# Attention and low-rank mixer on one core: diagonal score blocks first, key copies ahead of the cast of u, both transposed operands through ScalarE, the U-product in four column groups, a new order of the loop after the start-up

## The chip, the cores and the metric

The kernel runs on one core of a Trainium2 chip. The metric is device time in microseconds (us) of one execution; profiles are of one execution each, on the same kind of chip, and their span is about 2 us shorter than the time. Five engines matter: PE (TensorE matmul; PEld is its weight load), ACT (ScalarE), DVE (VectorE), POOL (GpSimd) and the DMA engines. In these traces each engine executes its own instructions in the order in which the program issues them, and this kernel sets that order by hand. "Slow clock" and "fast clock" are names for two durations that the same PE work shows: the six U-product matmuls of a pair take 0.82 us in the start-up of the kernel before and 0.50 us later.

## The reference, cut to what matters

```python
# q, k, v: (4, 8, 768, 64); local causal window of 96, 8 global keys, per-head slope
scores = q @ k.T / sqrt(64) + bias;  scores = where(keep, scores, -1e9)
a = softmax(scores);  attn = a @ v                       # -> x: (4, 768, 512)
h = (x.transpose(0, 2, 1) @ U) @ V                       # U: (768, 32), V: (32, 768)
u = x + h.transpose(0, 2, 1)
out = u + relu(u @ w_ch1) @ w_ch2                        # 512 -> 2048 -> 512
```

Heads are handled in 16 pairs, `i = 0 .. 15`, four pairs to a batch element. A query block of 128 needs its own key block (the diagonal block) and the block before it (the previous block), in which the first 32 columns are replaced by the global keys.

## The kernel before

Every pair goes through the same steps: transpose q and k on PE (`tp`/`tpb`), evacuate them (`qT`, `kT`), copy keys for the previous blocks (`kP`), scores in three chunks (`sc`), exp (`ep`), mask, AV product (`ob`), normalise (`x_sb`), cast (`x16`), U-product (`tmp_ps`), V-product (`h_ps`), add into `x_sb`, cast of u (`uu`), transpose u (`tpu`), copy (`uT`). Two-matrix MLP work (`hps`, `cps`) is cut into pieces and put between these steps by `fill(f)` once a batch element is complete.

```python
def k_prev(i, eng):                     # needs kT
    eng.tensor_copy(kP[:, :, G:P], kT[:, 0:NPB, G:P])
    eng.tensor_copy(kP[:, :, 0:G], kT[:, 0:1, 0:G].broadcast_to((P, NPB, G)))

# ... (1, t): block before, needs kP; (0, t): diagonal, needs only kT
ORDER = [(1, t) for t in range(1, NSB)] + [(0, t) for t in range(1, NSB)] + [(0, 0)]
CH = [list(range(0, 4)), list(range(4, 8)), list(range(8, 11))]

def mix_h(i, eng):
    hps = ps_ob("h_ps")                 # the same PSUM buffer as the AV product, bufs=1
    # ... six matmuls with V
    nc.vector.tensor_tensor(xp, xp, hps[...], ALU.add)
    eng.tensor_copy(uu, xp)             # the cast of u

# start-up loop, pairs 0 to 3 (no MLP work exists yet), cut:
    scores(i + 1, 0); av(i); norm(i); scores(i + 1, 1)
    if i > 0: mix_t(i - 1)
    cast_x(i); mask(i + 1, 0)
    transposes(i + 2, 0); mix_tmp(i); scores(i + 1, 2); transposes(i + 2, 1)
    mix_h(i, nc.vector if i == 0 else nc.gpsimd)
    mask(i + 1, 1)
    k_prev(i + 2, nc.vector if i == 0 else nc.gpsimd)

# loop after the start-up, pairs 4 to 15 (f MLP pieces in each gap), cut:
    scores(i + 1, 0); fill(f); av(i); norm(i); fill(f)
    scores(i + 1, 1); cast_x(i); fill(f)
    mask(i + 1, 0); transposes(i + 2, 0); fill(f)
    mix_tmp(i); scores(i + 1, 2); fill(f)
    mix_h(i, nc.gpsimd); fill(f)
    transposes(i + 2, 1); mask(i + 1, 1); k_prev(i + 2, nc.gpsimd); fill(f)
    # ... loads
    mix_t(i); fill(f)
```

The softmax here doesn't subtract the row's maximum and nothing guards it: scores larger than these inputs give would overflow.

## Time and profile before

The median of the kernel before is 291.75 us (290.54 to 291.88, four runs). I cut its profile at two events that the timeline shows: the first MLP matmul, and the start of the MLP matmuls that then run to the end without attention between them.

| Stage of the profile before | from, us | to, us | length, us |
|---|---|---|---|
| start-up (pairs 0 to 3, no MLP) | 0 | 58.68 | 58.68 |
| middle (pairs 4 to 15 with MLP pieces) | 58.68 | 228.52 | 169.84 |
| tail (MLP only) | 228.52 | 289.3 | 60.78 |

The windows view of the kernel before, one stretch from the start-up and one from the middle. The columns are stretch, its length, busy us and instructions of PE, PEld, DVE, ACT and POOL, then granted clock, DMA share and GB/s. The DMA share is above 1 in places and is not used here.

```profile
30.00:40.00 10.00, 6.20 (x84) 4.74 (x80) 5.63 (x9) 4.72 (x10) 3.90 (x5) 1.00 1.22 118
120.00:140.00 20.00, 19.92 (x163) 9.50 (x161) 9.76 (x15) 7.16 (x13) 5.14 (x6) 1.00 0.66 86
```

In the start-up PE is idle for almost four tenths of the time and no other engine is full either. That is the mark of a chain of dependences, not of a busy engine. In the middle PE is full.

The view of PE's waits of the kernel before (what PE waited for, us in total, times, longest us):

```profile
PE sc L265 <- POOL kP L226: 8.4, 3, 3.4
PE sc L265 <- DVE kP L226: 6.8, 3, 3.6
...
PE tmp_ps L336 <- ACT qT L211: 3.2, 6, 0.7
PE tmp_ps L336 <- DMA u_111<-in_moe_U_dram: 1.9, 1, 1.9
PE tpu L365 <- DVE kT L215: 1.2, 6, 0.2
```

The key copy is about half of all that PE waits for (15.2 of 31.3 us, the whole view summed). The chain that ended last shows what lies behind the copy (start us, us, what), in one start-up iteration of the kernel before:

```profile
32.89 0.77 DVE kT L215
...
33.77 0.95 DVE x_sb L353
...
34.78 1.35 POOL uu L357
36.13 0.59 POOL kP L225
36.72 0.27 POOL kP L226
...
37.04 0.28 PE sc L265
```

The key copy at 36.13 us needs only kT, whose evacuation ends at 33.85 us in the timeline. It stood in POOL's queue behind the cast of u, which itself stood behind the addition of h on DVE. So the scores of the next pair waited for the mixer of the previous one.

### The profile page before, as it was taken

The numbers are of one execution on the slowest core, as the hardware profiler recorded it, in microseconds if no ns is written. First come the engines' busy times: TensorE is split into PE (matmuls) and PEld (weight loads), VectorE is DVE, ScalarE is ACT, GpSimd is POOL, SyncE is SP. The second block draws the span as 40 slices with busy tenths as digits, with TensorE's granted clock in tenths as the row PEclk, the third lists the DMA queues.
The fourth block names the chain that finished last, engine by engine and source line by source line (L and its number), as shares of the span: only waits on it lengthen the run. The fifth ranks groups of instructions, "written<-read, shape, count | busy, mean of one in ns | idle before, by whom it ended". The sixth has DMA issues, their size and how long they took to land.

```text
span 289.3 us, 5035 instructions
## 1 busy us (share of the span) xinstructions
PE 252.7 (87%) x2144; PEld 129.0 (45%) x2144; DVE 149.3 (52%) x239; ACT 104.4 (36%) x185; POOL 61.2 (21%) x80
## 2 busy tenths in 40 slices
PE   2564585698899999999999999988999999999994
PEld 1343464454444444444444444544444444444441
DVE  5646736736665665564554635666655432123221
ACT  2753552444644234533146331446431032013100
POOL 8820137102430721060200701120301100000000
PEclk9999999999999999999999999999999999999998
DMA  8999979960971294039120291200011200210021
GB/s 86 176 191 211 175 98 192 191 71 6 125 64 39 30 207 107 2 39 162 73 81 4 21 180 73 69 18 2 0 39 37 75 0 0 75 73 0 0 73 74
DMA packets 47975, 22.68 MB, mean 78 GB/s; under 512 B 31408, under 2 KB 44368, under 8 KB 47952
## 3 DMA queue, kind: packets, MB, share of 16 engines
q0 software_dynamic: 36656, 13.73, 41.1%
q1 hardware_dynamic: 11296, 8.63, 10.2%
q8 instruction: 17, 0.28, 0.4%
q14 instruction: 6, 0.05, 0.1%
HBM read 27.46 MB, written 6.29 MB: 117 GB/s over the span
## 4 chain that ended last, share of the span: by engine, by line
PE 64%; DVE 11%; ACT 10%; POOL 8%; DMA 3%; issue 2%; POOLq 0%; DVEq 0%
PE cps L399 25%; PE hps L381 21%; PE sc L265 6%; ACT ep L270 4%; DVE kT L215 4%; DMA u_111<-in_moe_U_dram 3%; DVE x_sb L353 3%; PE tmp_ps L336 3%; POOL kP L225 3%; PE h_ps L348 2%; PE ob L303 2%; PE ob L307 2%; ACT qT L211 1%; POOL qkst L98 1%; POOL uu L357 1%
## 5 line engine op out<-in xcount | busy, mean ns | idle before, releaser
L381 PE MATMUL hps<-uT,w_16_81 128*128 128x512 f16 x384 | 94.1, 383 | 0.4
L399 PE MATMUL cps<-w_16_82,htr 128*128 128x512 f16 x384 | 90.4, 380 | 0.0
L270 ACT ACTIVATE ep<-sc 128x512 f16<-128x512 f32 (+1 forms) x96 | 48.7, 560 | 90.0 <-PE sc L265 90.0
L381 PEld LDWEIGHTS <-w_16_81 128*128 128x128 f16 x384 | 34.2, 98 | 40.2 <-issue 5.1
L399 PEld LDWEIGHTS <-htr 128*128 128x128 f16 x384 | 34.4, 98 | 38.5
L386 ACT ACTIVATE htr<-hps 128x512 f16<-128x512 f32 x48 | 28.7, 598 | 62.5 <-PE hps L381 61.9
L388 DVE TENSOR_SCALAR htr<-hps 128x512 f16<-128x512 f32 x48 | 33.0, 688 | 34.6 <-PE hps L381 34.6
L357 POOL CAST uu<-x_sb 128x768 f16<-128x768 f32 x14 | 13.1, 935 | 146.9 <-DVE x_sb L353 146.9
L406 DVE TENSOR_TENSOR osb<-cps,x_sb 128x512 f32<-128x512 f32 x24 | 16.6, 690 | 34.0 <-PE cps L399 34.0
L283 DVE TENSOR_TENSOR ep<-ep,expb 128x1280 f16<-128x1280 f16 x32 | 26.2, 818 | 7.4 <-ACT ep L270 7.4
L265 PE MATMUL sc<-qT,kP 64*128 64x128 f16 x160 | 11.6, 249 | 16.2 <-POOL kP L226 8.4
L353 DVE TENSOR_TENSOR x_sb<-x_sb,h_ps 128x768 f32<-128x768 f32 x16 | 15.2, 951 | 16.6 <-PE h_ps L348 16.6
L203 PEld LDWEIGHTS <-qkst 128*64 128x64 f16 x384 | 14.6, 130 | 15.8 <-issue 10.2
L265 PEld LDWEIGHTS <-kP 64*128 64x128 f16 x160 | 5.9, 104 | 27.6 <-POOL kP L226 13.0
L319 DVE RECIPROCAL rcp<-ob 128x12 f32<-128x12 f32 x16 | 3.7, 232 | 25.2 <-PE ob L307 25.2
L225 POOL COPY kP<-kT 128x480 f16<-128x480 f16 x13 | 13.0, 1000 | 15.4 <-DVE kT L215 15.4
L320 DVE TENSOR_TENSOR x_sb<-ob,rcp 128x768 f32<-128x768 f32 x16 | 15.3, 957 | 0.6
L303 PE MATMUL ob<-vp_85,ep 128*128 128x65 f16 x160 | 15.0, 209 | 0.0
L307 PE MATMUL ob<-v_84,ep 128*128 128x65 f16 x160 | 14.9, 209 | 0.0
L203 PE MATMUL tpb<-ident_93,qkst 128*64 128x128 f16 x144 | 10.0, 314 | 5.3 <-DMA qkst<-in_q_dram 4.8
L303 PEld LDWEIGHTS <-ep 128*128 128x128 f16 x160 | 13.1, 108 | 1.6 <-issue 0.3
L307 PEld LDWEIGHTS <-ep 128*128 128x128 f16 x160 | 13.2, 109 | 0.0
(112 smaller groups left out, 204.1 us busy)
## 6 DMA issues: line engine op xcount, KB each, us to landing
out_dram<-osb SPq DMA_DIRECT2D x24, 256.0 KB, 2.0
qkst<-in_q_dram POOLq DMA_DIRECT2D x7, 384.0 KB, 5.6
qkst<-in_k_dram POOLq DMA_DIRECT2D x7, 384.0 KB, 8.3
v_84<-in_v_dram POOLq DMA_DIRECT2D x7, 384.0 KB, 11.3
w_16_81<-in_moe_w_ch_dram POOLq DMA_DIRECT2D x2, 1024.0 KB, 15.8
w_16_82<-in_moe_w_ch_dram POOLq DMA_DIRECT2D x2, 1024.0 KB, 13.4
vp_85<-v_84 SPq DMA_DIRECT2D x14, 121.9 KB, 3.0
vp_85<-v_84 SPq DMA_DIRECT2D x28, 20.3 KB, 2.5
```

The costliest lines, as they stand in the source:

```text
L203: nc.tensor.matmul(tp[64 * hi:64 * hi + 64, sb * P:(sb + 1) * P], stg[:, hi, sb], ident16, is_transpose=True, start=(sb == 0), stop=(sb == ...
L225: eng.tensor_copy(kP[:, :, G:P], kT[:, 0:NPB, G:P])
L265: nc.tensor.matmul(scs[hi][:, j * P:(j + 1) * P], lhsT, qT[r, t * P:(t + 1) * P], start=(j == 0), stop=(j == n - 1),)
L270: nc.scalar.activation(ep[:, hi, idx[0]:idx[0] + n].rearrange("p n c -> p (n c)"), scs[hi][:, 0:n * P], AF.Exp, scale=qk_scale,)
L283: nc.vector.tensor_tensor(blk, blk, eb[:, :, m:m + 1].broadcast_to((P, 2, NPB, P)), ALU.mult,)
L303: nc.tensor.matmul(ob[:, t], ep[:, hi, t - 1], vp16[:, i % VPR, hi, t - 1], start=True, stop=False,)
L307: nc.tensor.matmul(ob[:, t], ep[:, hi, NPB + t - 1], v16[:, i % VR, hi, t], start=False, stop=True,)
L353: nc.vector.tensor_tensor(xp, xp, hps[:, 0:S].rearrange("p (n c) -> p n c", n=NSB), ALU.add)
L381: nc.tensor.matmul(hh, w1_16[:, dc, jt * P:(jt + 1) * P], uT[:, dc, t0:t0 + TT], start=(dc == 0), stop=(dc == NDC - 1),)
L386: nc.scalar.activation(htr[:, jt], hh, AF.Relu)
L388: nc.vector.tensor_scalar_max(htr[:, jt], hh, 0.0)
L399: nc.tensor.matmul(cps, htr[:, jc, tt * P:(tt + 1) * P], w2_16[:, jc], start=(jc == 0), stop=(jc == NJC - 1),)
```

## The change

The intent is to shorten that start-up chain and to make PE's own attention work shorter. The diff, cut to its core (a switch `DT` for transposes by DMA is also added, but it is off and changes nothing):

```diff
-    load(2, 2)
     u16 = ...; nc.gpsimd.dma_start(u16, moe_U...)
-    v16w = cst.tile([R, S], FP16, name="v16w")
-    nc.gpsimd.dma_start(v16w, moe_V)
+    v16w = cst.tile([P, S], FP16, name="v16w")         # V four times, one per column group
+    nc.gpsimd.dma_start(v16w[0:R], moe_V)
+    for g in range(1, NGR):
+        nc.sync.dma_start(v16w[g * R:(g + 1) * R], v16w[0:R])
+    load(2, 2)
@@ kT evacuation
-            nc.vector.tensor_copy(ko, tv)
+            if i == 0: nc.vector.tensor_copy(ko, tv)
+            else:      nc.scalar.activation(ko, tv, AF.Copy)
@@ block order (mask() and av() follow it)
-    ORDER = [(1, t) for t in range(1, NSB)] + [(0, t) for t in range(1, NSB)] + [(0, 0)]
+    ORDER = [(0, t) for t in range(1, NSB)] + [(0, 0)] + [(1, t) for t in range(1, NSB)]
@@ U-product
-                tmp_ps[0:R], u16[:, c], x16[:, c], start=(c == 0), stop=(c == NSB - 1),
+                tmp_ps[g * R:(g + 1) * R], u16[:, c], x16[:, c],      # g = c % 4
+                start=(c < NGR), stop=(c + NGR >= NSB), tile_position=(0, g * R),
@@ start-up loop
-            mix_h(i, nc.vector if i == 0 else nc.gpsimd)
-            mask(i + 1, 1)
-            k_prev(i + 2, nc.vector if i == 0 else nc.gpsimd)
+            k_prev(i + 2, nc.vector if i == 0 else nc.gpsimd)
+            mask(i + 1, 1)
+            mix_h(i, nc.vector)
@@ loop after the start-up
         av(i); norm(i)
+        transposes(i + 2, 0)
         fill(f)
         scores(i + 1, 1); cast_x(i); fill(f)
         mask(i + 1, 0)
-        transposes(i + 2, 0)
-        fill(f)
         mix_tmp(i)
+        fill(f)
         scores(i + 1, 2); fill(f)
         mix_h(i, nc.gpsimd)
-        fill(f)
+        mask(i + 1, 1)
         transposes(i + 2, 1)
-        mask(i + 1, 1)
         k_prev(i + 2, nc.gpsimd); fill(f)
         # ... loads
+        fill(f)
         mix_t(i)
```

The order of the loop after the start-up is rewritten too. Three moves in the start-up loop are cut from the diff as well: `mix_t(i - 1)` (the transposes of u and their copy) now comes behind the first mask instead of ahead of the cast of x, `v_prev(1)` comes earlier, and the last iteration has a new order of its own.

More of the change, by code (lines that the diff above doesn't have):

```diff
@@ L49 @@
     KEEP = False
+    DT = False
     assert NG <= G and NL <= P - G + 1 and NPAIR == NDC
@@ L89 @@
     NP = B * NPAIR
+    NSTART = NPAIR + 2
     stage = {}
@@ L112, in load_v, with load_qk_natural @@
         )
-    def load(i0, n):
-        load_qk(i0, n)
+    def load_qk_natural(i):
+        b, hp = divmod(i, NPAIR)
+        for which, src in enumerate((q, k)):
+            stg = stp.tile([P, NSB, 2, D], FP16, name="qkn", tag="qkn", bufs=4)
+            for hi in range(2):
+                nc.gpsimd.dma_start(
+                    stg[:, :, hi],
+                    src[b, 2 * hp + hi].rearrange("(n p) d -> p n d", p=P),
+                )
+            stage[i, which] = stg
+    def load(i0, n):
+        if DT and i0 >= NSTART:
+            for j in range(n):
+                load_qk_natural(i0 + j)
+        else:
+            load_qk(i0, n)
         load_v(i0, n)
@@ L145 @@
     load(1, 1)
-    load(2, 2)
     u16 = cst.tile([P, NSB, R], FP16, name="u16")
     nc.gpsimd.dma_start(u16, moe_U.rearrange("(c p) r -> p c r", p=P))
-    v16w = cst.tile([R, S], FP16, name="v16w")
-    nc.gpsimd.dma_start(v16w, moe_V)
+    NGR = P // R
+    v16w = cst.tile([P, S], FP16, name="v16w")
[3 more added lines that the diff above has]
+    load(2, 2)
     load_w1()
@@ L188 @@
     tmps = {}
-    NSTART = NPAIR + 2
     def transposes(i, which):
@@ L194, in transposes @@
         stg = stage.pop((i, which))
+        if DT and i >= NSTART:
+            dst = qkp.tile([P, NSB, P], FP16, name="qkT", tag="qT" if which == 0 else "kT")
+            nc.sync.dma_start_transpose(dst, stg.rearrange("p n h d -> p (n h d)"))
+            if which == 0:
+                qTs[i] = dst.rearrange("p n c -> p (n c)")
+            else:
+                kTs[i] = dst
+            return
         if i < NSTART:
@@ L214, in transposes @@
             kT = qkp.tile([P, NSB, P], FP16, name="kT", tag="kT")
-            nc.vector.tensor_copy(
-                kT.rearrange("p n c -> p (n c)").rearrange("p (c n) -> p c n", n=NSB), tv,
-            )
+            ko = kT.rearrange("p n c -> p (n c)").rearrange("p (c n) -> p c n", n=NSB)
+            if i == 0:
+                nc.vector.tensor_copy(ko, tv)
+            else:
+                nc.scalar.activation(ko, tv, AF.Copy)
             kTs[i] = kT
@@ L250, in scores @@
             return
-        qT, kT, kP = qTs[i], kTs[i], kPs[i]
+        qT, kT, kP = qTs[i], kTs[i], kPs.get(i)
         if ci == 0:
@@ L280, in mask @@
         eb = expb[:, 2 * hp:2 * hp + 2]
-        j0, m = ((0, 2), (NPB, 1))[part]
+        j0, m = ((0, 1), (NSB, 2))[part]
         blk = ep[:, :, j0:j0 + NPB]
@@ L285, in mask @@
         )
-        if part == 1:
+        if part == 0:
             nc.vector.tensor_tensor(
-                ep[:, :, NBK - 1], ep[:, :, NBK - 1], eb[:, :, 0], ALU.mult
+                ep[:, :, NPB], ep[:, :, NPB], eb[:, :, 0], ALU.mult
             )
@@ L298, in av @@
                     nc.tensor.matmul(
-                        ob[:, 0], ep[:, hi, NBK - 1], v16[:, i % VR, hi, 0],
+                        ob[:, 0], ep[:, hi, NPB], v16[:, i % VR, hi, 0],
                         start=True, stop=True,
@@ L303, in av @@
                 nc.tensor.matmul(
-                    ob[:, t], ep[:, hi, t - 1], vp16[:, i % VPR, hi, t - 1],
+                    ob[:, t], ep[:, hi, NSB + t - 1], vp16[:, i % VPR, hi, t - 1],
                     start=True, stop=False,
@@ L307, in av @@
                 nc.tensor.matmul(
-                    ob[:, t], ep[:, hi, NPB + t - 1], v16[:, i % VR, hi, t],
+                    ob[:, t], ep[:, hi, t - 1], v16[:, i % VR, hi, t],
                     start=False, stop=True,
@@ L335, in mix_tmp @@
         for c in range(NSB):
+            g = c % NGR
             nc.tensor.matmul(
-                tmp_ps[0:R], u16[:, c], x16[:, c], start=(c == 0), stop=(c == NSB - 1),
-            )
-        tmp16 = smp.tile([R, P], FP16, name="tmp16", tag="tmp16")
-        nc.vector.tensor_copy(tmp16, tmp_ps[0:R])
+                tmp_ps[g * R:(g + 1) * R], u16[:, c], x16[:, c],
+                start=(c < NGR), stop=(c + NGR >= NSB),
+                tile_position=(0, g * R),
+            )
+        tmp16 = smp.tile([P, P], FP16, name="tmp16", tag="tmp16")
+        nc.vector.tensor_copy(tmp16, tmp_ps)
         tmps[i] = tmp16
@@ L362, in mix_t @@
         uu = u16s.pop(i)
+        if DT and i >= NPAIR:
+            nc.sync.dma_start_transpose(
+                uT[:, hp, b * S:(b + 1) * S].rearrange("p (n c) -> p n c", n=NSB),
+                uu.rearrange("p n c -> p (n c)"),
+            )
+            return
         tpu = ps_tp("tpu", FP16, S)
@@ L442 @@
         scores(i + 1, 1)
+        cast_x(i)
+        mask(i + 1, 0)
+        if i == 0:
+            v_prev(1)
+        transposes(i + 2, 0)
         if i > 0:
             mix_t(i - 1)
-        cast_x(i)
-        mask(i + 1, 0)
-        if not last:
-            transposes(i + 2, 0)
-            mix_tmp(i)
-            scores(i + 1, 2)
-            transposes(i + 2, 1)
-            mix_h(i, nc.vector if i == 0 else nc.gpsimd)
+        mix_tmp(i)
+        scores(i + 1, 2)
+        if last:
+            mix_h(i, nc.vector)
+            mask(i + 1, 1)
+            transposes(i + 2, 1)
+            k_prev(i + 2, nc.gpsimd)
+            mix_t(i)
+        else:
+            transposes(i + 2, 1)
+            k_prev(i + 2, nc.vector if i == 0 else nc.gpsimd)
+            mask(i + 1, 1)
+            mix_h(i, nc.vector)
             if i + 2 < NPAIR:
                 masks_of(i + 2)
-            if i == 0:
-                v_prev(1)
-            mask(i + 1, 1)
-            k_prev(i + 2, nc.vector if i == 0 else nc.gpsimd)
-        else:
-            mix_tmp(i)
-            scores(i + 1, 2)
-            mix_h(i, nc.vector)
-            transposes(i + 2, 0)
-            transposes(i + 2, 1)
-            mix_t(i)
-            mask(i + 1, 1)
-            k_prev(i + 2, nc.gpsimd)
         if i == 0:
@@ L489 @@
         norm(i)
+        transposes(i + 2, 0)
         fill(f)
@@ L494 @@
         mask(i + 1, 0)
-        transposes(i + 2, 0)
+        mix_tmp(i)
         fill(f)
-        mix_tmp(i)
         scores(i + 1, 2)
         fill(f)
-        mix_h(i, nc.gpsimd)
-        fill(f)
+        mix_h(i, nc.vector if DT else nc.gpsimd)
+        mask(i + 1, 1)
         transposes(i + 2, 1)
-        mask(i + 1, 1)
         k_prev(i + 2, nc.gpsimd)
```

## The prediction

> **What bounds the kernel.** The windows view splits the 289.3 us profile. Up to 58.7 us (no MLP matmul yet) TensorE is busy 5.6 to 6.9 us of each 10; from 60 us on it is busy 93 to 100%, and the two MLP groups (94.1 + 90.4 us in the groups table) are work that the change does not touch. So about 20 us of idle TensorE lie before the first MLP matmul, only about 5 us after it.
>
> **The start-up loop.** Score groups that open with previous-block keys start at 26.47, 37.04, 47.62 and 58.14 us: a period of 10.57 us. The waits view: PE waits 8.4 us for the POOL key copy and 6.8 us for the DVE one, up to 3.6 us each time. In the timeline the hole is one serial tail: kT evacuation on DVE (0.96), x_sb addition (0.95), cast of u on POOL (1.35), key copy on POOL (about 0.95), then scores.
>
> **What the change does there.** Diagonal blocks need only kT, so the first chunk no longer waits for the key copy, which is next needed after the AV product. The cast goes to DVE (0.56) and the key copy runs beside the addition. kT moves to ScalarE (about 0.8, as the qT evacuations; ScalarE is about 45% busy here). A new chain remains, since AV and h_ps share one PSUM buffer. Adding traced durations from one AV start to the next: AV 1.4, normalise 1.2 beside scores 0.7 and exp 1.1, mask 0.8+0.3, uT copy 0.55 (it frees the bank that tmp_ps needs), tmp_ps 0.5, scores 0.4, exp 0.9, mask 0.8, addition 0.95: with hand-offs about 8.75 us. First iteration about 9.1, last about 9.8 to the first MLP matmul. With AV(0) at about 15.0 instead of 15.5, the first MLP matmul comes at about 51.4 us instead of 58.7: **7.3 us saved, all critical**. The 1.9 us wait of the first U-product for U goes (included). DMA is nearly saturated until 36 us; loads of pairs 4 to 7 become just-in-time.
>
> **U-product.** Six matmuls take 0.82 us (slow clock) or 0.50 us (fast). The Trainium skill, "TensorE: Matmul & The Clock Gate", Part 3, says matmuls in distinct column groups run concurrently (2.38x for three). Here the score matmuls, two row groups at once, show the like: 8 in 0.40 us. Estimate 0.3 us: 0.2 us saved x12. K = 128 instead of 32 for h_ps costs nothing.
>
> **Steady part.** The four 12.6 us iterations hold 0.7 us waiting for qT before the U-product and about 0.8 us for the key copy and kT. qT now comes early, but exp and cast still end about 0.9 us after PE is ready; the tail waits go. About 0.6 us each there, 0.1 to 0.5 us in the others, 0.2 us in the four dense iterations: **about 3.5 us**. The MLP tail (from 228.7 us) is unchanged.
>
> **Total.** 291.8 - 7.3 - 3.5 = **281 us**, 80% range 277 to 285.5. Faster by over 2% (below 286.0): 0.92; within 2%: 0.07; slower: 0.01.
>
> **What would show it.** First MLP matmul at 50 to 53 us; start-up period about 8.8 us; waits of scores for kP gone, small waits on ob (for the x_sb addition) and tmp_ps (for the uT copy or x cast) instead; U-product about 0.3 us fast; single-fill iterations about 12.0 us.
>
> **What would make it wrong.** ScalarE's longer queue delaying exp and mask more than added up; v_prev, q/k loads (pairs 4, 6) or the replicated V landing late, costing 1 to 3 us; column groups not overlapping; the tail being shorter than 8.75 us (down to 276).

## The result, and the profile after

The median after is 282.12 us (281.79 to 282.59, four runs) against 291.75 us. The ratio is 0.968, 95% interval 0.9649 to 0.9711. Ratios in this document are the mean time of one kernel's runs over that of the kernel before in the same rounds, so they are not quite the ratio of the medians that are quoted; one hundredth is about 2.9 us.

| Stage of the profiles | before, us | predicted, us | after, us |
|---|---|---|---|
| start-up, to the first MLP matmul | 58.68 | 51.4 | 50.12 |
| middle | 169.84 | about 166.3 (3.5 less) | 169.34 |
| tail | 60.78 | unchanged | 60.54 |

The total came out as predicted, but not its parts: the start-up gave 8.6 us where 7.3 were expected, the middle 0.5 us where 3.5 were expected.

The windows view after, the same two stretches:

```profile
30.00:40.00 10.00, 7.42 (x114) 5.52 (x114) 6.34 (x12) 7.54 (x14) 2.96 (x5) 0.98 1.57 186
120.00:140.00 20.00, 19.93 (x184) 10.23 (x184) 8.26 (x14) 6.47 (x12) 2.08 (x3) 1.00 0.64 104
```

In the start-up PE and ACT are both fuller. The view of PE's waits after:

```profile
...
PE tmp_ps L367 <- DVE uT L408: 3.6, 3, 1.3
PE tpu L404 <- POOL uu L390: 2.7, 8, 0.8
PE ob L333 <- DVE ep L313: 2.6, 1, 2.6
PE ob L328 <- DVE x_sb L386: 2.2, 3, 1.4
...
PE tmp_ps L367 <- ACT x_860 L359: 0.9, 1, 0.9
PE tmp_ps L367 <- ACT x_1042 L359: 0.9, 1, 0.9
PE tmp_ps L367 <- ACT x_1390 L359: 0.9, 1, 0.9
```

No line for kP is left. Two new kinds stand in the start-up, on the uT copy and on the addition, as predicted. A single wait of 2.6 us, of the first AV product for the mask, was not predicted; it is taken up under a2. In the middle there is one wait of 0.9 us for the cast of x in every iteration with one MLP piece per gap (seven such lines in all, three shown), where the kernel before had 0.7 us for qT in some of them and 0.2 us in others.

The chain after, in the start-up iteration that answers to the one shown before:

```profile
29.56 0.40 PE tmp_ps L367 x6
29.96 0.48 PE sc L295 x6
30.44 0.87 ACT ep L300 x2
31.36 0.71 issue
32.07 0.96 DVE x_sb L386
33.07 0.21 PE ob L328
```

"issue" here covers the mask on DVE (31.33 to 32.16 us in the timeline), after which DVE adds h. The next AV product needs the PSUM buffer that the addition frees. The key copy has left the chain.

### The profile page after: what moved, and what is told of

Same layout as the page of the kernel before. It is cut to its first block, busy times and chain, and to the rows that moved or that the text cites. A ratio compares the mean times of both kernels' runs of the same rounds, so it can differ in the third digit from the quotient of the medians.

```text
span 280.0 us, 5041 instructions
## 1 busy us (share of the span) xinstructions
PE 246.3 (88%) x2144; PEld 126.5 (45%) x2144; DVE 135.1 (48%) x226; ACT 116.4 (42%) x200; POOL 57.4 (21%) x78
## 4 chain that ended last, share of the span: by engine, by line
PE 70%; ACT 11%; DVE 9%; POOL 4%; issue 2%; DMA 2%; POOLq 0%; DVEq 0%; ACTq 0%
PE hps L420 27%; PE cps L438 25%; ACT ep L300 7%; PE sc L295 5%; DVE x_sb L386 4%; POOL uu L390 3%; PE tp L231 2%; PE ob L333 2%; PE tpu L404 2%; PE ob L337 2%; PE h_ps L381 2%; DVE ep L313 2%; DMA qkst<-in_q_dram 2%; PE tmp_ps L367 2%; PE ob L328 1%
## 5 line engine op out<-in xcount | busy, mean ns | idle before, releaser
L420 PE MATMUL hps<-uT,w_16_81 128*128 128x512 f16 x384 | 92.7, 382 | 0.4 <-ACT htr L425 0.4
L390 POOL CAST uu<-x_sb 128x768 f16<-128x768 f32 x12 | 15.1, 1261 | 133.4 <-DVE x_sb L386 133.4
L295 PE MATMUL sc<-qT,kT 64*128 64x128 f16 x192 | 13.0, 249 | 3.1 <-ACT kT L247 1.8
L408 DVE COPY uT<-tpu 128x768 f16<-128x768 f16 x16 | 8.9, 556 | 11.1 <-PE tpu L404 11.1
L255 POOL COPY kP<-kT 128x480 f16<-128x480 f16 x13 | 8.1, 625 | 26.2 <-ACT kT L247 26.2
```

The lines of the kernel that those rows point to most:

```text
L295: nc.tensor.matmul(scs[hi][:, j * P:(j + 1) * P], lhsT, qT[r, t * P:(t + 1) * P], start=(j == 0), stop=(j == n - 1),)
L420: nc.tensor.matmul(hh, w1_16[:, dc, jt * P:(jt + 1) * P], uT[:, dc, t0:t0 + TT], start=(dc == 0), stop=(dc == NDC - 1),)
```

## The experiments

All kernels below gave correct results and were timed in three rounds beside the kernel before. The table is of the profiled runs; the stages are cut as above. Times between kernels of different sets are compared by ratio. Each stage figure comes from one profiled execution, and executions of one kernel differ by up to 3.5 us (b1), so stage differences of about 1 us are readings of one profile and not settled.

| Kernel | start-up, us | middle, us | median, us | ratio to before (95%) |
|---|---|---|---|---|
| before | 58.68 | 169.84 | 291.75 | 1 |
| the change | 50.12 | 169.34 | 282.12 | 0.968 (0.9649, 0.9711) |
| a4: change, old block order | 51.06 | 172.67 | 286.08 | 0.9844 (0.9807, 0.988) |
| b1: change, cast of u ahead of key copy | 50.85 | 169.78 | 284.05 | 0.9782 (0.9719, 0.9846) |
| b2: before, new block order only | 52.61 | 167.35 | 282.71 | 0.973 (0.9692, 0.9768) |
| a3: change, kT on DVE | 52.49 | 171.60 | 286.19 | 0.9849 (0.9804, 0.9894) |
| a1: change, U-product in one group | 49.80 | 172.92 | 285.25 | 0.9808 (0.9744, 0.9872) |
| a2: a1, U and V loaded late | 51.33 | 172.47 | 287.27 | 0.9868 (0.9813, 0.9924) |
| b3: change, cast of x issued early | 49.73 | 161.54 | 273.58 | 0.9397 (0.9346, 0.9448) |
| b4: change, cast of u on DVE | 49.04 | 169.73 | 281.27 | 0.9669 (0.9617, 0.9722) |
| b5: change, old middle loop | 49.07 | 161.73 | 273.43 | 0.9392 (0.9363, 0.9421) |
| c2: b3 and an earlier uT copy | 49.33 | 163.64 | 274.94 | 0.9422 (0.9373, 0.9471) |
| c3: c2 and cast of u on DVE | 48.22 | 163.98 | 274.32 | 0.9409 (0.9362, 0.9456) |
| d1: c2, earlier loads, last two casts on DVE | 50.55 | 159.92 | 271.85 | 0.9333 (0.9284, 0.9381) |

### What made the start-up shorter

My theory was that the parts overlap: either taking kP out of the first scores or taking the cast out of the way of the key copy cures most of the wait. The rivals were that one part alone carries the gain, or that the unloading of DVE does.

**a4_prev_first**, the old block order in the changed kernel:

```diff
-    ORDER = [(0, t) for t in range(1, NSB)] + [(0, 0)] + [(1, t) for t in range(1, NSB)]
+    ORDER = [(1, t) for t in range(1, NSB)] + [(0, t) for t in range(1, NSB)] + [(0, 0)]
     # mask() and av() accordingly
```

> The changed kernel with the score blocks back in the old order (previous-block keys first), all else kept. My theory: with the key copy no longer behind the cast of u, it ends only about 0.9 us after kT, so the scores would wait about 0.9 us per start-up iteration but only about 0.5 us of it delays the AV product, which waits for the x_sb addition anyway: +2 us, about 284 us, first MLP matmul near 52 us. Rival (the diagonal order by itself is what brought the start-up gain): +6 us or more, about 288 us.

Measured: ratio 0.9844, a loss of 1.6 hundredths or about 4.8 us, between the theory and the rival. The start-up lost only 0.9 us, as the theory had it. The other 3.3 us came from the middle, which I had left out.

**b2_before_diag_only**, the new block order alone, on the kernel before:

> The kernel before with only the order of the score blocks changed. Theory: the parts overlap: the first scores no longer wait for the key copy, and the period of the start-up loop falls from 10.57 to about 8.6 us, set by kT copy, addition and mask on DVE: -6 us, about 286 us, although undoing the same part in the changed kernel costs only about 2 us. Rival (parts add up): the gain here equals the loss of the run that undoes the order, about 2 us, 290 us.

Measured: ratio 0.973, median 282.71 us. This one edit, without the rest, gives 2.7 of the 3.2 hundredths of the whole change. Its start-up is 6.1 us shorter, its middle 2.5 us. In the start-up the overlap is plain: the order is worth 6.1 us alone but costs 0.9 us when it is taken out of the whole, because the other edits shorten the same chain.

**b1_cast_ahead**, the cast of u again ahead of the key copy:

```diff
-            k_prev(i + 2, nc.vector if i == 0 else nc.gpsimd)
-            mask(i + 1, 1)
-            mix_h(i, nc.vector)
+            mix_h(i, nc.vector if i == 0 else nc.gpsimd)
+            mask(i + 1, 1)
+            k_prev(i + 2, nc.vector if i == 0 else nc.gpsimd)
```

> The changed kernel with the cast of u back on POOL ahead of the key copy in start-up iterations 1 and 2, and the mask of the second half after the addition. Theory: the key copy is needed only by the second score chunk, after AV, so it costs about 0.4 to 0.8 us in each of two iterations: +1 us, about 283 us. Rival (the place of the key copy is what brought the gain): +4 us or more.

Measured: median 284.05 us with a wide spread (282.46 to 285.96), so about 1 hundredth. The intervals of the ratios just miss each other (0.9711 and 0.9719) and the runs overlap (the change goes up to 282.59). The profile agrees with the theory in size: the two start-up iterations concerned took 8.80 and 8.79 us from one normalise to the next, against 8.13 and 7.85 us in the changed kernel. The time alone does not settle it.

**a3_kt_dve**, kT evacuated on DVE:

```diff
-            if i == 0: nc.vector.tensor_copy(ko, tv)
-            else:      nc.scalar.activation(ko, tv, AF.Copy)
+            nc.vector.tensor_copy(ko, tv)
```

> The changed kernel with kT evacuated on DVE again. Theory: in the start-up loop DVE carries the chain (mask, x_sb addition) into the next AV product, so 0.95 us more of DVE ahead of mask and addition lengthens each of four iterations by 0.7 to 0.95 us: +3.5 us, about 285.5 us. In the later part nothing. Rival (ScalarE is the limit since it took kT): the same or faster, 281 to 282 us.

Measured: ratio 0.9849, a loss of 1.7 hundredths or about 4.9 us. The start-up lost 2.4 us, less than the 3.5 expected, and the middle lost 2.3 us where I had expected nothing. ScalarE being the limit is ruled out.

**a2_u_late_one_group** and its partner **a1_one_group**. With U and V queued late, the copies of V would be late too, so both use one column group and differ only in the place of the two loads.

```diff
+    load(2, 2)
     u16 = cst.tile([P, NSB, R], FP16, name="u16")
     ...
-    load(2, 2)
     load_w1()
```

> As a1_one_group, and the loads of U and V back behind those of pairs 2 and 3 (one column group, so no replicas of V are needed in time). Theory: in the changed kernel the first AV product came late (16.6 us, behind a DVE copy), so U, which landed at about 20 us before, would be waited for by no more than 0.3 us: within 0.5 us of a1_one_group. Rival (the earlier load of U is part of the gain, as predicted: 1.9 us): +1.5 to +2 us over a1_one_group.

Measured: 287.27 against 285.25 us, 2.0 us slower in the same set, with no run of one among those of the other, though the intervals of the ratios overlap. My theory fell, and the rival's size holds. Its mechanism holds only in part. The U-product began at 20.12 us, when U had landed, against 19.23 us in a1; the cast of x had ended at 19.61 us, so only 0.5 us of that is due to U alone. The start-up grew by 1.5 us; 0.4 us of that stands before the first normalise (17.54 against 17.10 us) and 0.6 us after the fourth, and what causes these is not shown. The theory rested on a single profile, that of the change, in which the first AV product was late; in a1's it was over a microsecond earlier.

That lateness is worth a look. In the profile of the change the 32-partition copy of v on DVE ahead of the first AV product took 1.38 us, and in the kernel before 0.32 us. It took 1.38 us in two profiles (the change and a3), 0.70 us in b1, and 0.32 to 0.41 us in all others. In the two long cases the first normalise started at 17.98 us or later; in a1, with 0.41 us for the copy, it started at 16.83 us. POOL was issuing DMAs during both long copies, but it also did so all through the copy in a1 (0.41 us) and in b5 (0.32 us). So that alone does not make the copy long, and the cause stays open.

### What the U-product is worth

> The changed kernel with the U-product in one column group (6 matmuls into partitions 0 to 31, K = 32 for the product with V). Theory: 0.2 us per iteration after the start-up at the fast clock (12 of them), 0.4 us in each of four start-up iterations, all on PE's own path: +4 us, about 286 us. Rival (column groups do not overlap, or the time hides in waits): under +1 us.

The edit puts back the six matmuls into partitions 0 to 31 and the 32-row product with V. Measured: ratio 0.9808, a loss of 1.3 hundredths or about 3.7 us, nearly as expected. It lies in the middle (3.6 us). The lines of the groups view for the six matmuls of one pair, in the kernel before and in the change (busy us, mean ns of one, idle us before):

```profile
L336 PE MATMUL tmp_ps<-x_842,u_111 128*32 128x128 f16 x6 | 0.5, 218 | 0.7 <-ACT qT L211 0.7
```

```profile
L367 PE MATMUL tmp_ps<-x_860,u_106 128*32 128x128 f16 x6 | 0.3, 223 | 0.9 <-ACT x_860 L359 0.9
```

One matmul is not faster (218 and 223 ns). The six together take 0.29 us instead of 0.49 to 0.50 us in the timeline, because they overlap more closely. The same two lines also show that, in this pair, the wait ahead of the group grew by what the group saved.

### Where the gain of the middle went

After the start-up runs the open question was why the middle gave 0.5 us when b2, a3 and a1 say that block order, kT on ScalarE and column groups are each worth 2.3 to 3.6 us there. Something had to cost about as much.

**b3_cast_early**:

```diff
         fill(f)
-        scores(i + 1, 1)
         cast_x(i)
+        scores(i + 1, 1)
         fill(f)
```

> The changed kernel with one edit in the loop after the start-up: the cast of x is issued to ScalarE ahead of the exp of the second score chunk. Theory: the 0.93 us that PE waits for the cast before the U-product in the seven single-fill iterations (0.5 in the last) goes, and the later exp meets no tight wait: -5 us or more, about 276.5 us. Rival (another wait, on u or on the score banks, takes its place): under -2 us.

Measured: median 273.58 us, ratio 0.9397. Moving one line gained more than 8 us, nearly as much as the whole change, and more than the theory's 5 us. The reason shows in the timeline of ScalarE and PE. First the kernel with the change (start us, us, engine, line, operation, in brackets idle time before):

```profile
65.92 0.96 DVE L350 TENSOR_TENSOR x_sb<-ob,rcp 128x768 f32<-128x768 f32 x1
...
66.10 0.81 ACT L239 ACTIVATE qT<-tp 128x768 f16<-128x768 f16 x1 [0.47 <-PE tp L231]
...
67.40 1.08 ACT L300 ACTIVATE ep<-sc 128x512 f16<-128x512 f32 x2 [0.48 <-PE sc L295]
...
68.37 0.84 ACT L359 ACTIVATE x_1042<-x_sb 128x768 f16<-128x768 f32 x1
...
69.26 0.29 PE L367 MATMUL tmp_ps<-x_1042,u_106 128*32 128x128 f16 x6 [0.93 <-ACT x_1042 L359]
```

The same place in b3:

```profile
65.07 0.96 DVE L350 TENSOR_TENSOR x_sb<-ob,rcp 128x768 f32<-128x768 f32 x1
...
66.07 0.84 ACT L359 ACTIVATE x<-x_sb 128x768 f16<-128x768 f32 x1
...
66.82 1.06 ACT L300 ACTIVATE ep<-sc 128x512 f16<-128x512 f32 x2
...
67.42 0.29 PE L367 MATMUL tmp_ps<-x,u 128*32 128x128 f16 x6
```

In the change, x is normalised at 66.88 us (65.92 + 0.96) and ScalarE is idle from 66.91 to 67.40 us, yet the cast starts at 68.37 us. It is queued behind an exp whose scores come later. The Trainium skill, "TensorE: Matmul & The Clock Gate", Part 1 (engine queue depths), calls ScalarE and VectorE strict FIFO, and this is how it looks. In b3 the cast runs in that hole, and the exp comes only slightly later.

The single-piece iterations shrank from 12.37 to 11.30 us, from one normalise to the next. The iterations with two pieces per gap shrank too, from about 18.3 and 18.0 us to 17.9 us, and PE's busy time between 103.6 and 158 us (0.1 us left out) rose from 53.70 to 54.30 of 54.30 us; the 0.4 us of waits for ScalarE's relu in that stretch were gone. The theory had not counted those.

**b5_old_loop**, the loop of the kernel before in the changed kernel, all other parts kept:

> The changed kernel with the loop after the start-up in the order of the kernel before (U-product right before the third score chunk, query transposes after the mask, fills where they were). Theory: the new order of this loop is what eats the later gain: in it PE waits 0.93 us for the cast of x in all single-fill iterations, in the old order 0.7 us for qT in half of them and 0.2 in the rest, so the old order gains 0.3 to 0.6 us per iteration in about six iterations: 2 to 3 us faster than the change, about 279.5 us. Rival (kT on ScalarE or the column groups are what eats it): the same as the change, 282 us, or slower.

Measured: median 273.43 us, ratio 0.9392. The direction was right and the size three times too small. The order of the middle loop is what ate the gain, and the middle is now accounted for from the profiles:

| Step | middle, us | difference |
|---|---|---|
| before | 169.84 | |
| with the new block order only (b2) | 167.35 | -2.5 |
| with all parts but the new loop order (b5) | 161.73 | -5.6 |
| the whole change | 169.34 | +7.6 |

The middle term agrees with a1 and a3, which undo its two main parts one by one and lose 3.6 and 2.3 us, though they do so in the new order.

The old order has two MLP pieces between the second score chunk and the U-product. In b5 PE still waited there for qT, 3.2 us over six pairs. The new order has one piece, and so uncovered the cast in seven single-piece iterations and in the last pair. The early cast in the old order, which would join b3 and b5, was not tried.

**b4_u_cast_dve**, `mix_h(i, nc.vector)` in the middle loop:

> The changed kernel with the cast of u on DVE after the start-up too. Theory: PE waits 0.25 us for the POOL cast (1.3 us long beside DVE work) in single-fill iterations and more in the last two, 2.7 us in all; the DVE cast takes 0.56 us, so most of it goes: -2 us, about 280 us. Rival (DVE, with AV normalise, masks and relus, becomes late): no gain or a loss.

Measured: ratio 0.9669 against 0.968, the same. The waits for POOL's cast went from the list. In their place PE waited 1.8 us for relus on ScalarE (0.4 us in the change), 0.9 us for relus on DVE, and 1.4 us for the queries of pair 6. The rival was right, a wait moved.

Why POOL's cast had become a wait at all: it takes longer after the change. One line of the kernel before, then two of the change, from the timeline:

```profile
69.70 0.83 POOL L357 CAST uu<-x_sb 128x768 f16<-128x768 f32 x1 [11.61 <-DVE x_sb L353]
```

```profile
73.08 0.82 DVE L313 TENSOR_TENSOR ep<-ep,expb 128x1280 f16<-128x1280 f16 x1
73.23 1.35 POOL L390 CAST uu<-x_sb 128x768 f16<-128x768 f32 x1 [7.34 <-DVE x_sb L386]
```

The new order puts the mask, a DVE instruction with two SBUF inputs, directly beside the cast. The Trainium skill, "GPSIMD Engine Reference", Specifications, says that POOL shares its SBUF interfaces with VectorE and names two SBUF inputs as a case of contention. The trace agrees, with 0.83 us for the cast without the mask beside it and 1.35 us with it. The kernel before shows the same without any change of order: three of its casts on POOL began just after a mask and took 1.29 to 1.36 us, the other eleven took 0.83 us. In b5 four casts began ahead of the mask, and there it was the mask that took longer, 1.05 to 1.12 us instead of 0.82 us:

```profile
70.62 0.83 POOL L390 CAST uu<-x_sb 128x768 f16<-128x768 f32 x1 [6.67 <-DVE x_sb L386]
71.08 1.05 DVE L313 TENSOR_TENSOR ep<-ep,expb 128x1280 f16<-128x1280 f16 x1
```

So in these traces the one of the two that begins second is the one that takes longer. After the change the key copy ran faster, 625 ns in the mean of its larger part against 1000 ns.

### Trying for more

**c2_cast_and_ut_early** issues the transposes of u ahead of the first mask in the start-up loop:

```diff
         cast_x(i)
-        mask(i + 1, 0)
-        ...
         transposes(i + 2, 0)
         if i > 0: mix_t(i - 1)
+        mask(i + 1, 0)
```

> b3_cast_early plus one edit in the start-up loop: the transposes of u and their copy into uT are issued ahead of the first mask on DVE. Theory: PE waits about 1.2 us for that copy before the U-product in three start-up iterations; freeing the bank earlier saves about 0.6 us in each, until the cast of x is the next limit: about 1.8 us under b3_cast_early, 271.8 us. Rival (the chain through the mask and the addition on DVE is the limit either way): the same as b3, 273.5 us.

This puts `mix_t` back ahead of the mask, near where the kernel before had it. Measured: 0.9422, not faster than b3. The edit did what it should (the waits for the uT copy fell from 3.0 us in b3 to 1.9 us, and an iteration of 7.6 us appears), and the start-up is 0.4 us shorter, but the middle is 2.1 us longer. The wait for the queries of pair 6 does not explain that: it was 0.6 us, against 1.1 us in b3. After it PE was slower: the twelve transposes of those queries took 0.85 us (0.53 us in b3), and the first two groups of four MLP matmuls 1.89 and 1.69 us (1.04 us each in b3). What sets off this slow stretch is not shown. **c3_all** adds the cast on DVE:

> c2_cast_and_ut_early plus the cast of u on DVE after the start-up. Theory: the 2.2 us of PE waits for the POOL cast go: about 1.5 us under c2, 270.3 us. Rival (relus on DVE become late, as the waits of b4_u_cast_dve show: 2.7 us for htr copies): the same as c2 or slower.

Measured: 0.9409, the same. Its start-up is the shortest, 48.22 us, and its middle is longer by 2.4 us than b3's. It has the slow stretch too (1.89 and 1.52 us), and this line among PE's waits:

```profile
PE tp L231 <- DMA qkst<-in_q_dram: 2.2, 1, 2.2
```

The query transposes of pair 6 began at 53.07 us in c2, after a wait of 0.6 us, and at 52.97 us in c3, after one of 2.2 us. In the change PE got there at 53.15 us and did not wait. So the load lands near 53 us however early PE arrives, and the shorter start-ups of c2 and c3 gained nothing.

**d1_best** issues the loads of pairs 6 and 7 one iteration earlier than the second MLP weights and casts u on DVE in the last two iterations only:

```diff
         if i == 1:
-            load_w2()
-        if i == 2:
             load(6, 2)
+        if i == 2:
+            load_w2()
```

> c2_cast_and_ut_early with the loads of pairs 6 and 7 issued one iteration earlier, ahead of the second MLP weights, and the cast of u on DVE in the last two iterations only. Theory: the shorter start-up of c2 and c3 was lost at the first query transposes of pair 6, which waited for a load that lands near 53 us whatever PE does; with the load earlier that wait goes (2.2 us in c3, 1.1 us in b3) and the slow-clock stretch after it shortens, and the last two iterations save about 1 us: about 271 us, no PE wait for query loads after 40 us. Rival (the load is not the limit, the slow clock at the start of the MLP is): within 1 us of c2 and c3, 274 us. A second risk: the MLP weights land late, and the first output products wait.

Measured: median 271.85 us, ratio 0.9333, the lowest of all. It beats both kernels clearly. Its interval overlaps with those of b3 and b5, so its lead over them is not settled. Half of the theory held. The wait for queries of pair 6 and the slow stretch after it are gone (1.04 us for the four MLP matmuls), and the last pair's iteration took 9.65 us instead of 10.41 us in b3. But the start-up of the profiled run, which was the slowest of its four, was not shorter; another DMA had become the wait:

```profile
PE ob L333 <- DMA vp<-v: 1.5, 2, 1.3
```

With this much DMA in flight, moving one load ahead delayed another. What order of loads is best there is left open.

## Why the prediction was right or wrong

**The total: right.** 281 us was predicted, 282.12 us measured, and the chance of 0.92 was put on the right side. That it came so close is partly luck: the start-up gave 1.3 us more than forecast and the middle 3.0 us less.

**What bounds the start-up: right.** The waits for kP are gone, waits for the x_sb addition (2.2 us) and for the uT copy (3.6 us) stand in their place, with a smaller one for kT (1.8 us) and one for the mask ahead of the first AV product (2.6 us), which the prediction did not have.

**The size of the start-up gain: 7.3 us predicted, 8.6 us measured.** The mis-sized term is the period of the new chain. "With hand-offs about 8.75 us" was measured as 8.13 and 7.85 us, and the first iteration, put at 9.1 us, as 8.36 us. The durations named in the prediction add up to 7.8 us, so it allowed 0.95 us for hand-offs, where 8.13 us leaves about 0.3 us. Part of the shorter period is that one iteration ran a stretch of its matmuls at the fast clock (the U-product at 37.68 us took 0.29 us instead of 0.40 us). Against that, the first AV product did not run at 15.0 us: all but its first matmul waited until 16.62 us in this profile, behind the slow copy of v.

**The load of U: right in size, the mechanism only in part.** The wait was put at 1.9 us; undoing the earlier load cost 2.0 us (a2), but in that profile only 0.5 us of it is directly the wait for U.

**The U-product: right.** "About 0.3 us" was 0.29 us, and undoing it cost 3.6 us in the middle, more than the 0.2 us x 12 of the prediction. The product with V did not get longer with K = 128 (0.50 us for six matmuls in both). The Trainium skill, "TensorE: Matmul & The Clock Gate", Part 3, agrees in kind; its 2.38x is for three matmuls in three groups, while six in four groups gave 0.50/0.29, about 1.7x.

**The middle: wrong.** The step that failed is "The four 12.6 us iterations hold 0.7 us waiting for qT ... the tail waits go. About 0.6 us each there, 0.1 to 0.5 us in the others". Single-piece iterations were to take 12.0 us and took 12.37 us. The prediction knew that "exp and cast still end about 0.9 us after PE is ready", and 0.93 us was measured; but it set this off against the 0.7 us of the four worst iterations, and took the rest to gain as well. The iteration that took 12.06 us before now also took 12.37 us, and the last pair's went from 10.71 to 11.38 us. It also held that the tail waits would go, but the cast on POOL, beside the mask, became a new one of 0.25 us in single-piece iterations.

The deeper miss is that the predicted gain of the middle was a sum over waits of one schedule. It never asked what the new parts would give in the old order. They give 8.1 us there (169.84 to 161.73), and the rewritten order takes 7.6 us back.

**DMA just in time: right as a risk.** No load delayed the change after the transposes of pairs 0 and 1. c3 shows that the next gain in the start-up would have met one.

## What to carry to other kernels

In a hand-ordered program, look in each engine's queue for an instruction that is ready while the engine idles for the one in front of it; here moving one such cast forward was worth nearly as much as the whole change. When a change bundles new parts with a new order, test the parts in the old order, since one can hide the other. Undoing a part and doing it alone measure different things when several parts cut the same chain: the block order was worth 6.1 us of start-up alone, and 0.9 us as the last part taken out.

## What the Trainium skill lacked or had wrong

- "TensorE: Matmul & The Clock Gate", Part 1, describes a half-rate clock until PE has been busy for some microseconds. The start-up agrees in direction: in the kernel before, the q and k transposes took 314 ns each there and 223 ns later, and the first four MLP matmuls 1.89 us together against 1.04 us a little later. The page warns that clock events in a trace can be unreliable. A case that it does not have is the kernel before, where the granted clock reads 1.00 all through the start-up.
- "TensorE: Matmul & The Clock Gate", Part 3, gives speedups for groups used once each. For six matmuls of 128 columns in four groups, two of them used twice, the runs show 0.29 us against 0.50 us.
